# Gate logits from the tenth tile on: outputs as the stationary operand, eight moving columns, summed in place

## The chip, the cores and the metric

The kernel runs on one core of one Trainium2 chip. The metric is the device time of one execution in microseconds (us); less is better.

## The reference, cut to what matters

Two stages follow each other. A gated linear attention runs over a sequence of 768 tokens for each of 4 x 8 heads, and its output, seen as 3072 tokens of 384 numbers, goes through a layer of eight experts, of which each token takes the one with the largest logit.

```python
state = alpha[:, :, t, :, None] * state + k_t v_t          # for each of 768 tokens t
y[:, :, t] = einsum('bhd,bhde->bhe', q[:, :, t], state)
x = y.transpose(0, 2, 1, 3).reshape(3072, 384)
logits = x @ w_gate + modality_bias[modality_id]           # 8 logits for each token
e_idx = argmax(logits, axis=1)
gate_w = softmax(logits)[e_idx]
out[mask] = gate_w * (relu(x[mask] @ w1[e]) @ w2[e])       # for each expert e
```

The change is in `x @ w_gate`.

## The kernel before, in words

The 3072 tokens are 24 tiles of 128. The attention works on two tiles at once: there are 12 pairs, and a loop over s (line 946) has one step for each pair. A step is a software pipeline. In step s the scans of pair s run on VectorE and GpSimd (`back`, `totals`, `forth`, `scaled_keys`, `scaled_queries`), while TensorE makes the scores of pair s - 1 (`scores`), turns its keys (`keys`), and, for pair s - 2, whose outputs have been copied from PSUM to the tile `yt` (`outputs`), turns the outputs into rows for the store (`rows`) and makes the gate logits. Then come `from_state` (queries times the state, tile names qh and UB), `states` (the new state, written to the PSUM tile `kv`) and `from_values` (scores times values, scT and vt). The order on every engine is the order in which the code is written; nothing is moved by a scheduler.

In `yt` the outputs lie turned: head dimension on the partitions, 128 tokens along a row, four blocks j of two heads each, for each of the two tiles c of a pair. The gate weights `wgp` are laid out in the same way, four blocks of 128 x 32 of which 8 columns are filled.

The logits take two stages. `logits_turned` (line 403) makes four matmuls, one for each block j: the weights block (32 columns) is stationary, the outputs of both tiles (256 columns) move, and each result goes to its own 32 partitions of a PSUM bank. ScalarE copies the bank to `lts` (line 408). The four partial sums still have to be added and turned. For the first ten tiles (pairs 0 to 4, `TURNED` = 10) `turn_logits` and a reduction on VectorE do that. For the later tiles (pairs 5 to 11) `add_logits` (line 425) does it with one matmul for each tile: `lts` is stationary and `fold`, a 128 x 8 matrix of ones and zeros made on VectorE at the start (line 200), moves; the result is 8 columns of `LP`, a part of the same PSUM bank as `kv`.

Pairs 5 to 9 get their logits in steps 7 to 11. Pairs 10 and 11 get theirs in the code after the loop, where l = 11 (lines 1091 to 1130): `logits_turned(l - 1)` stands before `from_state(l)` and `add_logits(l - 1)` behind it; `logits_turned(l)` is called between the two halves of the first block of the first expert (line 1123, tiles xHL and w1H, w1L), and `add_logits(l)` after `rows(l)`.

From LP the routing reads the logits on VectorE (`route_group`, tile room), counts tokens per expert on TensorE (`rank_counts`, tiles oh, tri, ones) and from that come the places of the tokens and the choice of the expert weights to load. Behind it 12 blocks of 256 tokens go through the experts.

The PSUM tiles `b` rotate over five banks; `logits_turned` takes one of them in each step. `st[s, "yt"]` has two buffers.

Of the kernel before, what the change touches and what calls it, by code (L numbers as in the profile page):

```python
# [8 lines left out]
F32 = mybir.dt.float32  # L9
# [5 lines left out]
ALU = mybir.AluOpType  # L15
AF = mybir.ActivationFunctionType
AX = mybir.AxisListType
# [4 lines left out]
P = 128  # L22
B, H, S, D = 4, 8, 768, 48
NC = S // P
NP = H // 2
SEG = P + 1
DM = H * D
E = 8
# [26 lines left out]
TURNED = GROUPS[0][1]  # L55
# [20 lines left out]
def attention_moe(ctx: ExitStack, tc: tile.TileContext, q, k, v, alpha, at_, kt_, qt_, vt_, mid, wg, wgp_, mb, w1, w2, out):  # L76
    nc = tc.nc
    order = [1]
    vec, act, pool, pe, sp = (Ordered(e, tc, order) for e in (nc.vector, nc.scalar, nc.gpsimd, nc.tensor, nc.sync))
# [6 lines left out]
    ident = cp.tile([P, P], F32, name="ident")  # L86
# [3 lines left out]
    ac = actx.enter_context(tc.tile_pool(name="ac", bufs=1))  # L90
# [24 lines left out]
    st = {}  # L115
# [14 lines left out]
    def small(p, *shape):  # L130
        return ps.tile([p, *shape], F32, name=next_bank())

    def load(s, names="akqv"):
        z = {"0": slice(0, NP), "1": slice(NP, KS)}.get(names[-1], slice(0, KS))
        for n in names:
            if n == "a":
                c = slice(z.start and z.start * SEG + 1, z.stop * SEG + 1)
                sp.dma_start(X[s % NX_][:, c], at_[s, :, c])
            elif n in "kq":
                sp.dma_start((KT if n == "k" else QT)[s % NB][:, z], (kt_ if n == "k" else qt_)[s, :, z])  # L140
            elif n == "v":
                sp.dma_start(VT[s % NV][:, : 2 * DM], vt_[s])
# [3 lines left out]
    wgp = cp.tile([P, NP, 32], F32, name="wgp")  # L146
# [11 lines left out]
    LP = kvl[:, KS * D :].rearrange("p (t e) -> p t e", e=E)  # L158
# [37 lines left out]
        UB.append(t)  # L196
    bhi = ac.tile([P, 1], F32, name="bhi")
    vec.memset(bhi, -float(ALPHA_MAX_BITS))
    fold = ac.tile([P, E], F32, name="fold")
    vec.tensor_reduce(fold, ident.rearrange("p (j e) -> p e j", e=32)[:, :E], axis=AX.X, op=ALU.add)  # L200
    gacc = ac.tile([P, PS], F32, name="gacc")
    amin = ac.tile([P, PS, KS], F32, name="amin")
    junk = ea.tile([P, KS * SEG + 1], BF16, name="junk")
# [46 lines left out]
    def back(s, z):  # L250
        x, G = X[s % NX_], st[s, "G"]
        r = slice(z.start * SEG + 1, z.stop * SEG + 1)
        vec.tensor_tensor_scan(G[:, r][:, ::-1], x[:, r][:, ::-1], DR[:, ::-1], 0.0, op0=ALU.mult, op1=ALU.max)

    def totals(s, z):
        r = slice(z.start * SEG + 1, z.stop * SEG + 1)
        vec.reciprocal(DF[:, 0::SEG], st[s, "G"][:, r][:, 0::SEG])
# [5 lines left out]
    def scaled_keys(s, z, engine):  # L263
        engine.tensor_tensor(st[s, "k"][:, z], KT[s % NB][:, z], seg(st[s, "G"][:, 1:], 1, z), op=ALU.mult)
# [4 lines left out]
    def begin(s):  # L269
        st[s, "G"] = sb.tile([P, KS * SEG + 1], F32, name="G")  # L270
        st[s, "F"] = ea.tile([P, KS * SEG], F32, name="Fw", bufs=1)
        st[s, "k"] = sb.tile([P, KS, P], F32, name="kh")
        st[s, "q"] = sb.tile([P, KS, P], F32, name="qh")
# [110 lines left out]
    def outputs(s, zs=(0, 1)):  # L384
        if 0 in zs:
            st[s, "yt"] = sb.tile([P, 2, NP, P], F32, name="yt")
        for z in zs:
            act.copy(st[s, "yt"][:, z], st[s, "yp"][z])
# [14 lines left out]
    def logits_turned(s):  # L403
        lt = small(P, 2, P)
        for j in range(NP):
            pe.matmul(lt[32 * j : 32 * j + 32], wgp[:, j], st[s, "yt"][:, :, j], start=True, stop=True)
        l2 = sb.tile([P, 2, P], F32, name="lts")
        act.copy(l2, lt)
        st[s, "l"] = l2
# [14 lines left out]

    def add_logits(s):
        for c in range(2):
            pe.matmul(LP[:, 2 * s + c - TURNED], st[s, "l"][:, c], fold, start=True, stop=True)

    def logits_pe(i, xs, wgs):
        xt = bank(ND, P)  # L430
# [459 lines left out]
    def run(s, phase):  # L890
        for f, a in later.pop((s, phase), ()):
            f(*a)
# [44 lines left out]
    def do(steps):  # L937
        for f in steps:
            f[0](*f[1:])

    def warm(n):
        w = bank(NP, P)
        for i in range(n):
            pe.matmul(w[:, i % NP], ident, ident, start=True, stop=True)

    for s in range(PS):
        if 0 < s and s + 1 < PS:
            load(s + 1, "kqv")
        if 0 <= s - 2:
            outputs(s - 2)  # L950
        late, by = [], vec
        if s == 0:
            warm(14)
            begin(0)
            for z in ZS:
                back(0, z)
                scaled_keys(0, z, pool)
                totals(0, z)
                forth(0, z)
                scaled_queries(0, z, pool if z == Z0 else vec)  # L960
        elif s == 1:
            begin(1)
            scores(0, 0)
            for z in range(2):
                turn_keys(0, z)
                if z == 0:
                    warm(2)
            back(1, Z0)
            scaled_keys(1, Z0, pool)
            scores(0, 1)  # L970
            totals(1, Z0)
            forth(1, Z0)
            scaled_queries(1, Z0, pool)
            back(1, Z1)
            scaled_keys(1, Z1, pool)
            totals(1, Z1)
            forth(1, Z1)
            scaled_queries(1, Z1)
        else:
            if (s - 1, "S") not in st:  # L980
                state(s - 1)
            decayed(s - 1)
            run(s, "state")
            for z in range(2):
                scores(s - 1, z)
            run(s, "masks")
            todo = scans(s)
            if len(todo) > 1:
                late = todo.pop()
            if s >= 4:  # L990
                by = pool
            for f in todo:
                do(f)
            run(s, "counts")
        if 1 < s:
            keys(s - 1)
        if 0 <= s - 2:
            rows(s - 2)
        if 0 <= 2 * (s - 3) < TURNED:
            turn_logits(s - 3)  # L1000
        if 0 <= s - 2:
            logits_turned(s - 2)
        run(s, "small")
        if 0 <= 2 * (s - 3) < TURNED:
            sum_logits(s - 3)
        run(s, "middle")
        do(late[:-1])
        if 0 <= s - 1:
            from_state(s - 1)
        if 0 <= s - 1 and (s - 1) % NC == 0:  # L1010
            states(s - 1)
        if TURNED <= 2 * (s - 2):
            add_logits(s - 2)
        if 0 <= s - 1 and (s - 1) % NC:
            states(s - 1)
        run(s, "sums")
        for f, *x in late[-1:]:
            f(*x, by)
        if 0 <= s - 1:
            from_values(s - 1)  # L1020
        run(s, "end")
        for c in range(s - (s < 5), s + 1 - (s < 4)):
            if 0 <= c < PS:
                guard(c)
        if 0 <= s - 2:
            store(s - 2)
        for c in range(s + 2 + (s > 4), s + 3 + (s > 3)):
            if c < PS:
                load(c, "a")
        if s == 0:  # L1030
            sp.dma_start(wgp, wgp_)
        if s == 1:
            sp.dma_start(mi.rearrange("p t w -> p (t w)"), mid.bitcast(I32))
            sp.dma_start(mbb, mb.unsqueeze(0).broadcast_to([P, NM, E]))
        if s == 2:
            sp.dma_start(xd[MID : MID + 1], of[0:1])
            sp.dma_start(gd[MID : MID + 1], of[0:1, 0:1])
# [37 lines left out]
    def first_block(i, w1, between=None, low_last=False):  # L1075
        xH, xL = XH[i % 2], XL[i % 2]
        wH, wL = w1
        hp = bank(2, T)
        for z in range(2):
            if z and between:  # L1080
                between()
            fs = slice(z * P, (z + 1) * P)
            terms = [[(wH, xH, d), (wL, xH, d), (wH, xL, d)] for d in range(ND)]
            terms = [t for u in terms for t in u]
            if low_last:
                terms.sort(key=lambda t: t[1] is xL)
            for n, (w, x, d) in enumerate(terms):
                pe.matmul(hp[:, z], w[:, d, fs], x[:, d], start=(n == 0), stop=(n == len(terms) - 1))
        return hp

    l = PS - 1
# [4 lines left out]
    w1s = [w1_part(0, 0)]  # L1096
# [3 lines left out]
    slot_tables()  # L1100
    out_of_range()
    rows(l - 1)
    logits_turned(l - 1)
    gate_rows(0, EARLY[0])
    gather_gates(0, row(EARLY[0]))
    store(l - 1)
    with tc.issue_after(sp.last):
        weights(0, 0, (1,))
    from_state(l)
    add_logits(l - 1)  # L1110
    prep(0, False)
    from_values(l)
    route_group(*t[0])
# [6 lines left out]
    rank_masks(*t[0])  # L1120
    w1s += [w1_part(0, 1)]
    outputs(l, (1,))
    hp = first_block(0, w1s[0], lambda: logits_turned(l), True)
    rank_split(*t[0])
    keys_early(1)
    half_index()
    w1s += [w1_part(0, 2)]
    rows(l)
    store(l)
    add_logits(l)  # L1130
    route_places(*t[0])
    act.activation(hf[0], hp, AF.Relu)
    route_group(*t[1])
# [1 line left out]
    hp = first_block(0, w1s[1])  # L1135
# [3 lines left out]
    hp = first_block(0, w1s[2])  # L1139
# [9 lines left out]
    hp = first_block(0, w1s[3], last_counts)  # L1149
# [146 lines left out]
    w1s = []  # L1296
    for u in range(2):
        us = slice(u * P, (u + 1) * P)
        op = py.tile([P, 512], F32, name=f"y{u}")[:, :DM]
        for f in range(NF):  # L1300
            j, z = divmod(f, 2)
# [18 lines left out]
    for i in range(1, NS0):  # L1320
        w1s = slot(i, w1s)
# [90 lines left out]
```

## Time and profile before

| | us |
|---|---|
| runs, as listed | 343.24, 549.6, 344.5 |
| median of the runs | 344.5 |
| the profiled execution | 343.79 |
| its span, from the first to the last instruction | 342.1 |
| TensorE busy (share of the span) | 330.8 (97%) |
| weight loads of TensorE | 300.7 (88%) |
| VectorE busy | 265.7 (78%) |
| ScalarE busy | 229.5 (67%) |
| GpSimd busy | 170.8 (50%) |
| mean granted clock of TensorE, full = 1 | 0.996 |

In the profile's rows PE is TensorE's matmul, PEld its weight load (the two overlap), DVE is VectorE, ACT is ScalarE, POOL is GpSimd. Times are counted from the start of the span. A row of the timeline has the start, the time from the first start to the last end of the instructions merged in it, and their count. One matmul of plain f32 operands shows as two weight loads and two matmul records; a transpose shows as one of each. The matmuls overlap their neighbours, and their ends are modelled, so the time that a group of matmuls takes from the engine is read from its start to the start of the next group, which is called its slot here. All instructions that the recording helper issues have line L66, so the tiles' names tell them apart.

### The profile page before, as it was taken

The page shows a single profiled execution, that of the slowest core. Times are in us where ns is not written, and L with a number is a line of the kernel's source. Part 1 is how long each engine was busy: PE and PEld are TensorE (multiplying, and loading weights), DVE is VectorE, ACT ScalarE, POOL GpSimd, SP SyncE. Part 2 cuts the span into 40 slices and gives each one's busy share as a digit, 9 for nine tenths or more (in the row PEclk, how much of TensorE's full clock was granted, in tenths as well). Part 3 has the DMA queues.
Part 4 walks back from the last instruction along what each step waited for, and adds up shares of the span by engine and source line. Part 5 has one row for each costly group of instructions (what it writes and reads, how often), then busy time and mean ns, then how long its engine had stood idle before and what let it go on. Part 6 is the DMA issues. An engine that isn't in the chain of part 4 may idle for free. (4 is left out here: it accounts for less than half of the span.)

```text
span 342.1 us, 8364 instructions
## 1 busy us (share of the span) xinstructions
PE 330.8 (97%) x3162; PEld 300.7 (88%) x3162; DVE 265.7 (78%) x487; ACT 229.5 (67%) x454; POOL 170.8 (50%) x185
## 2 busy tenths in 40 slices
PE   6899999999999999999999999999999999999991
PEld 6788888888888977999999999999898989898990
DVE  6999999999985876959696868686878777787430
ACT  1767978767686516858585868686868676767430
POOL 7778799788767047554252524251444252411021
PEclk9999999999999999999999999999999999999998
DMA  7998899986185956997867676667586767660010
GB/s 231 398 398 297 288 321 321 327 297 248 44 283 148 375 215 229 372 383 253 258 217 231 210 248 225 227 223 219 164 295 219 223 209 246 205 208 23 1 50 32
DMA packets 39799, 80.07 MB, mean 234 GB/s; under 512 B 3867, under 2 KB 20404, under 8 KB 39748
## 3 DMA queue, kind: packets, MB, share of 16 engines
q1 hardware_dynamic: 35652, 69.38, 58.8%
q0 software_dynamic: 4096, 10.05, 8.9%
q8 instruction: 27, 0.44, 0.5%
q14 instruction: 24, 0.20, 0.2%
HBM read 69.77 MB, written 9.65 MB: 232 GB/s over the span
## 5 line engine op out<-in xcount | busy, mean ns | idle before, releaser
L66 PE MATMUL b<-xHL,w1H 128*128 128x512 f32 (+1 forms) x312 | 102.6, 378 | 0.0
L66 POOL DMA_INDIRECT out_dram<-os,idx x25 | 27.2, 1087 | 110.4 <-ACT os L66 70.8
L66 PE MATMUL b<-xHL,w1L 128*128 128x256 f32 x288 | 80.6, 280 | 0.0
L66 PEld LDWEIGHTS b<-xHL,w1H 128*128 128x128 f32 x312 | 57.4, 188 | 11.3 <-issue 0.4
L66 PE MATMUL y<-w2H,hH 128*128 128x384 f32 x184 | 62.6, 340 | 0.0
L66 PE MATMUL y<-w2H,hL 128*128 128x384 f32 x184 | 61.7, 335 | 0.0
L66 PE MATMUL y<-w2L,hH 128*128 128x384 f32 x184 | 61.6, 335 | 0.0
L66 DVE TENSOR_TENSOR hs<-b,low 128x256 f32<-128x256 f32 x88 | 33.9, 415 | 32.6 <-ACT low L66 32.6
L66 PEld LDWEIGHTS b<-xHL,w1L 128*128 128x128 f32 x288 | 54.2, 188 | 0.1
L66 DVE TENSOR_TENSOR w1L<-w1r,w1H 128x768 fp32r<-128x768 f32 x48 | 43.8, 951 | 6.6 <-ACT w1H L66 6.3
L66 DVE TENSOR_TENSOR w2L<-w2r,w2H 128x768 fp32r<-128x768 f32 x48 | 45.8, 958 | 3.4 <-ACT w2H L66 3.4
L66 ACT ACTIVATE os<-y,gg 128x384 f32<-128x384 f32 x25 | 14.6, 583 | 39.7 <-PE y L66 39.7
L66 ACT CAST w2H<-w2r 128x768 fp32r<-128x768 f32 x48 | 40.0, 841 | 0.0
L66 ACT COPY low<-b 128x256 f32<-128x256 f32 x88 | 30.1, 367 | 14.5 <-PE b L66 14.5
L66 POOL DMA_INDIRECT xg<-xd,idx x26 | 29.4, 1130 | 18.7 <-DVE idx L66 11.0
L66 ACT CAST w1H<-w1r 128x768 fp32r<-128x768 f32 x48 | 37.9, 839 | 0.8 <-ACT ls L66 0.8
L66 POOL DMA_INDIRECT gg<-gd,idx x26 | 28.7, 1103 | 18.7 <-issue 13.1
L66 PEld LDWEIGHTS y<-w2L,hH 128*128 128x128 f32 x184 | 34.6, 188 | 0.0
L66 PEld LDWEIGHTS y<-w2H,hH 128*128 128x128 f32 x184 | 34.6, 188 | 0.0
L66 PEld LDWEIGHTS y<-w2H,hL 128*128 128x128 f32 x184 | 34.5, 188 | 0.0
L66 ACT COPY scT<-b 128x512 f32<-128x512 f32 x48 | 24.8, 599 | 14.2 <-PE b L66 13.1
L66 POOL TENSOR_TENSOR kh<-kt,G 128x512 f32<-128x512 f32 x24 | 30.5, 1278 | 6.3 <-DVE G L66 5.7
(180 smaller groups left out, 593.7 us busy)
## 6 DMA issues: line engine op xcount, KB each, us to landing
w1r<-in_w_dram SPq DMA_DIRECT2D x26, 768.0 KB, 5.4
w2r<-in_w_dram SPq DMA_DIRECT2D x26, 768.0 KB, 5.8
X<-in_turned_alpha_dram SPq DMA_DIRECT2D x10, 516.5 KB, 5.3
kt<-in_turned_k_dram SPq DMA_DIRECT2D x10, 512.0 KB, 5.5
qt<-in_turned_q_dram SPq DMA_DIRECT2D x10, 512.0 KB, 6.6
vt<-in_paired_v_dram SPq DMA_DIRECT2D x12, 384.0 KB, 6.2
xd<-xs SPq DMA_DIRECT2D x12, 384.0 KB, 4.9
kt<-in_turned_k_dram SPq DMA_DIRECT2D x4, 256.0 KB, 2.8
```

The costliest lines, as they stand in the source:

```text
L66: ins = f(*a, **kw)
```

## The change

`add_logits` makes the logits of a tile in one stage. For each of the two tiles c it issues four matmuls, one for each block j, into the same 8 columns of `LP`: the outputs `yt[:, c, j]` (128 x 128) are stationary, 8 columns of the weights block move, and PSUM adds the four. `fold` goes away, and for pairs 5 to 11 so do `logits_turned`, its bank and ScalarE's copy to `lts`. The call stands where `logits_turned` stood: in steps 7 to 11 right after `rows`, that is before `from_state` and `states`; after the loop before `gate_rows` and `from_state(l)` for pair 10, and in the middle of the first expert block for pair 11. Pairs 0 to 4 keep their stages.

```diff
-    fold = ac.tile([P, E], F32, name="fold")
-    vec.tensor_reduce(fold, ident.rearrange("p (j e) -> p e j", e=32)[:, :E], axis=AX.X, op=ALU.add)
...
     def add_logits(s):
         for c in range(2):
-            pe.matmul(LP[:, 2 * s + c - TURNED], st[s, "l"][:, c], fold, start=True, stop=True)
+            for j in range(NP):
+                pe.matmul(
+                    LP[:, 2 * s + c - TURNED], st[s, "yt"][:, c, j], wgp[:, j, :E], start=(j == 0), stop=(j == NP - 1)
+                )
...
-        if 0 <= s - 2:
+        if 0 <= 2 * (s - 2) < TURNED:
             logits_turned(s - 2)
+        if TURNED <= 2 * (s - 2):
+            add_logits(s - 2)
...
-        if TURNED <= 2 * (s - 2):
-            add_logits(s - 2)
         if 0 <= s - 1 and (s - 1) % NC:
             states(s - 1)
...
     rows(l - 1)
-    logits_turned(l - 1)
+    add_logits(l - 1)
...
     from_state(l)
-    add_logits(l - 1)
...
-    hp = first_block(0, w1s[0], lambda: logits_turned(l), True)
+    hp = first_block(0, w1s[0], lambda: add_logits(l), True)
...
     store(l)
-    add_logits(l)
```

TensorE in step 7, the first that changes, before: the partial logits stand ahead of the new state (kv from vt and knat), and the folding behind it.

```order
L66 MATMUL b_1126<-ident,lts 128x128 x2
L66 MATMUL b_1129<-yt,wgp 32x256 x4
L66 MATMUL kv<-vt_89,knat 64x48 x16
L66 MATMUL kv<-fold,lts 128x8 x2
L66 MATMUL b_1141<-scT,vt_89 64x128 x8
```

And now:

```order
L66 MATMUL b_1124<-ident,lts 128x128 x2
L66 MATMUL kv<-wgp,yt 128x8 x8
L66 MATMUL kv<-vt_89,knat 64x48 x16
L66 MATMUL b_1140<-scT,vt_89 64x128 x8
L66 MATMUL b_1141<-scT,vt_89 64x128 x8
```

Four matmuls of 256 columns and two of 8 have become eight of 8 columns, and all stand ahead of the new state.

TensorE after the loop, pair 11, inside the first expert block (b from xHL and the weights w1H, w1L), before:

```order
L66 MATMUL b_2014<-xHL_107,w1H 128x256 x3
L66 MATMUL b_2024<-yt,wgp 32x256 x4
L66 MATMUL b_2014<-xHL_107,w1H 128x256
L66 MATMUL b_2014<-xHL_107,w1L 128x256
L66 MATMUL b_2014<-xHL_107,w1H 128x256
L66 MATMUL b_2014<-xHL_107,w1L 128x256
L66 MATMUL b_2014<-xHL_107,w1H 128x256
L66 MATMUL b_2014<-xHL_107,w1L 128x256
L66 MATMUL b_2014<-xHL_107,w1H 128x256 x3
L66 MATMUL b_2061<-ident,yt 128x128 x4
L66 MATMUL b_2067<-ident,yt 128x128 x4
L66 MATMUL kv<-fold,lts 128x8 x2
```

And now:

```order
L66 MATMUL b_2006<-xHL_107,w1H 128x256 x3
L66 MATMUL kv<-wgp,yt 128x8 x8
L66 MATMUL b_2006<-xHL_107,w1H 128x256
L66 MATMUL b_2006<-xHL_107,w1L 128x256
L66 MATMUL b_2006<-xHL_107,w1H 128x256
L66 MATMUL b_2006<-xHL_107,w1L 128x256
L66 MATMUL b_2006<-xHL_107,w1H 128x256
L66 MATMUL b_2006<-xHL_107,w1L 128x256
L66 MATMUL b_2006<-xHL_107,w1H 128x256 x3
L66 MATMUL b_2054<-ident,yt 128x128 x4
L66 MATMUL b_2060<-ident,yt 128x128 x4
```

The final logits of pair 11 are complete before the second half of that block; the folding behind the transposes of yt is gone.

## Rows read from the trace of the kernel before

**Rows 1.** Page, part 1: busy us (share of the span), instructions.
```profile
PE 330.8 (97%) x3162; PEld 300.7 (88%) x3162; DVE 265.7 (78%) x487; ACT 229.5 (67%) x454; POOL 170.8 (50%) x185
```

**Rows 2.** Busy time by stretch: attention and routing; the expert blocks.
```profile
core 0: us, PE busy (x) PEld busy (x) DVE busy (x) ACT busy (x) POOL busy (x), PEclk, DMA share, GB/s
17.00:125.00 108.00, 108.00 (x1762) 93.90 (x1761) 96.37 (x203) 76.67 (x166) 78.56 (x82) 1.00 0.80 282
...
140.00:330.00 190.00, 190.00 (x1135) 179.54 (x1134) 141.58 (x234) 135.20 (x258) 66.06 (x60) 1.00 0.64 214
```

**Rows 3.** Timeline of PE, step 7.
```profile
start us, us, engine line op out<-in xcount [idle before <-releaser]
...
60.80 0.64 PE L66 MATMUL b<-yt,wgp 128*32 128x256 f32 x8
61.37 1.14 PE L66 MATMUL kv<-vt,knat 128*64 128x48 f32 x32
62.44 0.61 PE L66 MATMUL kv<-fold,lts 128*128 128x8 f32 x4
62.98 0.33 PE L66 MATMUL b<-scT,vt 128*64 128x128 f32 x2
```

**Rows 4.** Timeline of PE after the loop: pair 10, then pair 11.
```profile
104.75 0.64 PE L66 MATMUL b<-yt,wgp 128*32 128x256 f32 x8
105.31 0.28 PE L66 MATMUL b<-ident,gt 128*16 128x128 f32 x1
...
106.56 0.61 PE L66 MATMUL kv<-fold,lts 128*128 128x8 f32 x4
107.02 0.30 PE L66 MATMUL b<-ident,xg 128*128 128x128 f32 x1
...
111.19 0.64 PE L66 MATMUL b<-yt,wgp 128*32 128x256 f32 x8
111.76 0.38 PE L66 MATMUL b<-xHL,w1H 128*128 128x256 f32 x1
...
113.81 0.51 PE L66 MATMUL kv<-fold,lts 128*128 128x8 f32 x4
114.17 0.36 PE L66 MATMUL b<-xHL,w1H 128*128 128x256 f32 x1
```

**Rows 5.** Timeline of PEld: folding in step 7, token table in step 11.
```profile
62.44 0.52 PEld L66 LDWEIGHTS kv<-fold,lts 128*128 128x128 f32 x4
...
96.84 0.47 PEld L66 LDWEIGHTS <-OL 128*128 128x128 f16 x16 [0.41 <-DVE OHE L66]
```

**Rows 6.** Groups by tile, 60 to 115 us: busy us, mean ns | idle before.
```profile
L66 PEld LDWEIGHTS kv<-fold,lts 128*128 128x128 f32 x28 | 3.7, 190 | 0.9 <-issue 0.7 <-ACT lts L66 0.2
L66 ACT COPY lts<-b 128x256 f32<-128x256 f32 x7 | 3.2, 454 | 1.1 <-PE b L66 1.1
```

**Rows 7.** Timeline of PE, steps 2 and 3: transposes before another array split, and before their like.
```profile
18.87 1.04 PE L66 MATMUL b<-ident,yt 128*128 128x128 f32 x8
19.83 0.64 PE L66 MATMUL b<-yt,wgp 128*32 128x256 f32 x8
...
27.18 1.04 PE L66 MATMUL b<-ident,yt 128*128 128x128 f32 x8
28.06 0.38 PE L66 MATMUL b<-ident,lts 128*128 128x128 f32 x2
```

**Rows 8.** Timeline, step 8: VectorE's last read of kv, TensorE's partial logits.
```profile
66.85 0.55 DVE L66 COPY S<-kv 128x384 f32<-128x384 f32 x1
...
68.76 0.64 PE L66 MATMUL b<-yt,wgp 128*32 128x256 f32 x8
```

**Rows 9.** Timeline of PE, step 11: scores; stretch after TensorE's last matmul.
```profile
92.39 2.06 PE L66 MATMUL b<-qh,kh 48*128 48x128 f32 x32
94.38 1.09 PE L66 MATMUL b<-ident,kh 128*128 128x128 f32 x8
...
338.00:342.10 4.10, 0.00 (x0) 0.00 (x0) 0.00 (x0) 0.00 (x0) 0.00 (x0) 0.65 0.03 7
```

## Prediction

> **What bounds the kernel now.** I read the page's shares first: TensorE has the largest, 97% of the span [rows 1]. A busy share can mislead, because matmuls are pipelined and their ends are modelled, so I went on to the busy time by stretch. From 17 to 125 us, where all of the change lies, TensorE is busy for 108.00 of 108.00 us, and from 140 to 330 us for 190.00 of 190.00 [rows 2]. VectorE has 96.37 of the 108 and is a close second. What settles it is the timeline of TensorE: each group of matmuls begins where the one before it leaves off, with no idle bracket, and the same group takes the same slot wherever it stands. The partial logits take 0.57 us in step 7 (60.80 to 61.37) and 0.57 us after the loop (111.19 to 111.76) [rows 3, 4]. An engine that waited now and then for VectorE, a bank or a transfer would show uneven slots. So TensorE's stream of matmuls sets the pace all the way, the expert blocks begin when it gets there, and what a step adds to or takes from the stream arrives at the end one for one. The reader is to see two things: the matching slots, and that nothing else in the program has to change for the time to change.
>
> **What goes.** In steps 7 to 11 the partial logits take 0.57 us and the folding 0.54 us (62.44 to 62.98) [rows 3]; the row of step 7 stands for five equal ones. That is 5 x 1.11 = 5.55 us. For pair 10 it is 0.56 us (104.75 to 105.31) and 0.46 us (106.56 to 107.02); for pair 11 it is 0.57 us and 0.36 us (113.81 to 114.17) [rows 4]. Together 5.55 + 1.02 + 0.93 = 7.50 us leave TensorE's stream.
>
> **What comes.** Each of seven pairs gets eight matmuls of 128 x 128 stationary and 8 moving columns in f32. The trace before has this very shape: the folding, 128*128 with 128x8. Its two matmuls show as four weight loads and four records, so eight will show as sixteen. The four loads last 0.52 us from first start to last end [rows 5], and one load lasts 190 ns [rows 6], so a load starts (0.52 - 0.19) / 3 = 0.11 us after the one before. That weight load is the price; the 8 columns pass beside it. Sixteen of them take 16 x 0.11 = 1.76 us, and seven pairs 7 x 1.76 = 12.32 us. Put simply, the old form loaded little and moved much (weights of 32 columns, four side by side in the array), the new one loads much and moves little, and here loading is the dearer part.
>
> Bounds for the one load, since sixteen in a row of this form do not stand in the trace: the nearest row below is the token table's, f16 128*128, sixteen loads in 0.47 us, 0.03 us each [rows 5]; above is a load that overlaps nothing, 0.19 us [rows 6]. By the lower, seven pairs take 3.4 us, by the upper 21.3. I take 0.11, the row of the same type and shape.
>
> **Edges between groups.** The eight transposes of `yt` take 0.96 us when the partial logits follow, which split the array into four (18.87 to 19.83), and 0.88 us when full-width transposes follow (27.18 to 28.06) [rows 7]. The new matmuls are full width, so the edge before them costs about 0.09 less, seven times: -0.63 us. Behind them, the folding's slot of 0.54 is 0.10 more than four times 0.11, where a split group follows; the new block has such a follower in steps 7 and 9: +0.2 us. Elsewhere full-width or small groups follow, and `from_state` now passes straight into `states`, an edge that I set to nothing between 0 and 0.1.
>
> **The sum.** 12.32 + 0.2 - 7.50 - 0.63 = +4.4 us. Against the profiled execution, 343.79 us (a span of 342.1 and 1.7 around it), that gives 348.2 us. This execution lies between the two undisturbed runs, 343.24 and 344.5, so it serves as the median too. With the lower bound of the load the sum is -4.5 us (339.3), with the upper +13.4 us (357.2).
>
> **What I cost at nothing.** ScalarE loses seven copies to `lts`, 3.2 us [rows 6], but TensorE does not wait for ScalarE in these steps, so nothing is gained. The reduction for `fold` at the start goes, on VectorE, before its first scan; nothing is late for it. The logits of a pair are final before `from_state` instead of behind it, which lets VectorE's routing start sooner, but TensorE reaches the counts no sooner. One bank fewer in the rotation of five only loosens waits. One wait is new: the first of the eight matmuls writes to the bank of `kv`, and so waits for VectorE's last read of it. In step 8 that read ends at 66.85 + 0.55 = 67.40 and the matmul would start near 68.7, 1.3 us later [rows 8]. The whole of TensorE is queued behind that matmul; were the cover gone, each us of lateness would cost a us. TensorE getting slower widens it.
>
> **Rivals.**
>
> The load goes at the short pace, and the change gains. The matmul has only 8 columns to move, and if the stationary operand could be taken in as the f16 table is, 0.03 us for each [rows 5], the time would be 339.3 us. For it: that row is real, and the same engine does it. Against: the folding, in f32, has 0.11 four times over, and the operand here is f32. The Trainium skill, "TensorE: Matmul & The Clock Gate", section "Back-to-back issue gap", gives a floor of about 25 ns for an isolated matmul of few columns, which would speak for this rival, but says that in a stream of loads and matmuls both set the spacing; the folding's row agrees with the second.
>
> TensorE is not the bound, and the added time is hidden: 343.8 us, no difference. For it: VectorE is busy for 96.37 of 108 us [rows 2], and PE's ends are modelled, so TensorE's wait could be hidden in overlaps. Against: the equal slots. It would need slots that shrink when the matmuls come earlier.
>
> The clock falls, and the kernel is slower by more than 2%. In steps 8, 10 and 11 there would stand, one after the other, the transposes of keys and of outputs, eight each (0.88 us for eight [rows 7]), and 1.76 us of matmuls with few columns: some 3.5 us with little moving, against 1.8 us now before the partial logits, which move 256 columns each. The granted clock does fall in this trace: it is 0.65 on average from 338 to 342 us, where TensorE has nothing to do [rows 9]. If it fell to the lower of its two levels (1.2 against 2.4 GHz) in one such step while the values and scores pass, the scores alone, 1.99 us (92.39 to 94.38) [rows 9], would take twice that, and the values, of like length, too: about +3.9 us a step. One full fall gives 352.1 and decides it; five give 367.7. Against: the clock is 1.00 over all stretches with work [rows 2], and TensorE is never idle. The same page, section "Part 4: PE-mode transpose", says that transposes do not count as activity in the way that matmuls do. No run here shows that; by it this rival gets a little more weight, still a small one.
>
> **How the numbers follow.** The forecast, 348.2 us, gets 0.87. The clock gets 0.05, the hidden cost 0.05, the short load 0.03. A measurement of this kernel tells about 2% from no change, 6.9 us, so from 337.6 to 351.4 us is the middle class. The forecast lies in it at +1.3%, the hidden cost and the short load's 339.3 too; of the latter I put 0.02 beyond the edge, since its 0.03 us counts the last load's whole length in. Of the forecast 0.03 goes to the upper side, for waits at the new place. So faster 0.02, same 0.90, slower 0.08. The range is 345.5 to 351.0 us: below, it takes in a load that overlaps a little better and half of the hidden case; above, a load of 0.13 us or edges twice as dear.
>
> **What would show it.** Right: each of the seven blocks of eight matmuls shows sixteen loads at 0.11 us and a slot of 1.75 to 1.9 us, TensorE still fills its stretch, the scores' slot is still 1.99 us, and the first expert block starts about 4.4 us later with all behind it moved by as much. Wrong: a slot of the block under 1 us (short load), idle brackets on TensorE or unequal slots (a wait has taken over), a granted clock under 1.00 between 60 and 115 us, or a later part that takes up the delay.

## Result and the profile after

The changed kernel takes 347.64 us (median of 4 runs, 345.95 to 349.69). The kernel before has a median of 343.87 us over four runs; one of them, 549.6 us, stands far from all others, and the ratio leaves it out. The other three have a median of 343.24 us, and against them the changed kernel takes 1.0127 times as long, with a 95% interval of 1.0099 to 1.0155. Run a second time among the experiments it gave 1.010 (1.0068 to 1.0132). It is slower by a little over 1%, which the rule of 2% calls no change, and the interval lies clear of 1. The prediction was 348.2 us, a ratio of 1.013.

The first thing to look at is where TensorE's time went. This is its timeline in step 7 of the changed kernel, the same stretch as [rows 3]:

```profile
60.19 0.38 PE L66 MATMUL b<-ident,lts 128*128 128x128 f32 x2
60.41 1.85 PE L66 MATMUL kv<-wgp,yt 128*128 128x8 f32 x16
62.19 1.14 PE L66 MATMUL kv<-vt,knat 128*64 128x48 f32 x32
63.16 0.51 PE L66 MATMUL b<-scT,vt 128*64 128x128 f32 x6
```

Eight matmuls show as sixteen records, and their slot is 60.41 to 62.19, 1.78 us, where partial logits and folding took 0.57 and 0.54. Step 11 and the two places after the loop, the latter beside [rows 4]:

```profile
97.87 1.85 PE L66 MATMUL kv<-wgp,yt 128*128 128x8 f32 x16
99.58 0.54 PE L66 MATMUL b<-OHE,OL 128*128 128x2 f16 x16
...
106.83 1.85 PE L66 MATMUL kv<-wgp,yt 128*128 128x8 f32 x16
108.53 0.27 PE L66 MATMUL b<-ident,gt 128*16 128x128 f32 x1
...
113.86 1.85 PE L66 MATMUL kv<-wgp,yt 128*128 128x8 f32 x16
115.57 0.36 PE L66 MATMUL b<-xHL,w1H 128*128 128x256 f32 x1
```

Here the slots are 1.71, 1.70 and 1.71 us. The loads, beside [rows 5] and [rows 6], from PEld's timeline in step 7 and from the groups by tile between 60 and 118 us:

```profile
60.30 1.87 PEld L66 LDWEIGHTS kv<-wgp,yt 128*128 128x128 f32 x16
```

```profile
L66 PEld LDWEIGHTS kv<-wgp,yt 128*128 128x128 f32 x112 | 13.1, 192 | 0.0
```

Sixteen loads in 1.87 us, each of 0.192: (1.87 - 0.19) / 15 = 0.112 us from one to the next. The busy time by stretch, beside [rows 2]:

```profile
core 0: us, PE busy (x) PEld busy (x) DVE busy (x) ACT busy (x) POOL busy (x), PEclk, DMA share, GB/s
17.00:128.00 111.00, 111.00 (x1787) 101.36 (x1784) 95.81 (x202) 74.45 (x159) 79.45 (x83) 1.00 0.78 274
143.00:333.00 190.00, 190.00 (x1134) 179.50 (x1134) 141.69 (x234) 135.25 (x257) 68.49 (x61) 1.00 0.65 216
```

TensorE still fills every stretch and its clock is full. PEld's busy time in the first stretch has grown from 93.90 to 101.36 us, in a stretch 3 us longer: what the change adds is loading.

A good measure of the whole is TensorE's own way from one fixed group to its last matmul, because it leaves out the start (first loads from memory) and the end (last store), which vary from run to run. From the transposes of `yt` in step 2 to the last matmul of the last expert block, the kernel before and then the changed kernel. For the latter a row between stands here too, the first expert block behind the last changed group, which in [rows 4] starts at 114.17 us:

```profile
18.87 1.04 PE L66 MATMUL b<-ident,yt 128*128 128x128 f32 x8
...
334.29 0.34 PE L66 MATMUL y<-w2H,hL 128*128 128x384 f32 x1
```

```profile
18.57 1.04 PE L66 MATMUL b<-ident,yt 128*128 128x128 f32 x8
...
117.52 0.37 PE L66 MATMUL b<-xHL,w1H 128*128 128x256 f32 x1
...
337.64 0.34 PE L66 MATMUL y<-w2H,hL 128*128 128x384 f32 x1
```

The way is 315.42 us before and 319.07 us after: +3.65 us. This is the effect of the change as TensorE sees it, 1.1% of the time, and the measured ratios agree with it. All of it arises up to the row between: from there to the last matmul TensorE takes 220.12 us in both kernels (114.17 to 334.29, 117.52 to 337.64), so the expert blocks pass the delay on one for one. The profiled execution's own time rose by only 345.95 - 343.79 = 2.2 us; its start was 0.30 us earlier (18.57 against 18.87), and the stretch from the last matmul's start to the end of the span 1.3 us shorter (6.5 against 7.8). The end is not touched by the change. At the start the reduction for `fold` is gone, but the same row starts at 18.57 to 19.18 us in the runs below that have no `fold` either, so the 0.30 us are within what varies.

### The profile page after: what moved, and what is told of

The parts are those of the page before. It is cut to its first block, busy times and chain, and to the rows that moved or that the text cites. A ratio compares the mean times of both kernels' runs of the same rounds, so it can differ in the third digit from the quotient of the medians.

```text
span 344.1 us, 8411 instructions
## 1 busy us (share of the span) xinstructions
PE 335.0 (97%) x3190; PEld 309.1 (90%) x3190; DVE 265.5 (77%) x486; ACT 227.7 (66%) x447; POOL 172.2 (50%) x185
## 4 chain that ended last, share of the span: by engine, by line
PE 91%; DVE 3%; DMA 2%; issue 1%; SPq 0%; ACT 0%; POOL 0%; POOLq 0%; DVEq 0%
PE b L66 54%; PE y L66 30%; PE kv L66 8%; DMA X<-in_turned_alpha_dram 1%; DVE Fw L66 1%; DVE G L66 1%; DMA out_dram<-os,idx 1%; DVE qh L66 1%; SPq L66 0%; POOL out_dram L66 0%; DVE room L66 0%; ACT os L66 0%; POOLq L1324 0%; ACT hH L66 0%; DVEq L66 0%
## 5 line engine op out<-in xcount | busy, mean ns | idle before, releaser
L66 POOL DMA_INDIRECT xg<-xd,idx x26 | 31.3, 1205 | 20.9 <-DVE idx L66 11.0
L66 ACT COPY scT<-b 128x512 f32<-128x512 f32 x48 | 24.8, 598 | 13.9 <-PE b L66 13.4
```

The costliest lines, as they stand in the source:

```text
L66: ins = f(*a, **kw)
```

## Experiments

**The block once more, in the same place.** Each pair's eight matmuls are issued twice. This prices sixteen loads and asks whether added work is hidden.

```diff
-        for c in range(2):
+        for c in (0, 1, 0, 1):
             for j in range(NP):
                 pe.matmul(
```

> The changed kernel with each block of eight logit matmuls issued a second time into the same columns (same result). If TensorE's stream sets the pace and a 128x128 f32 weight load costs 0.11 us, each of seven pairs gets sixteen more loads, 16 x 0.11 = 1.78 us: all that stands behind moves by 7 x 1.78 = 12.4 us more than in the changed kernel, the time is about 360 us (ratio 1.047 to 1.052 to the kernel before), and the scores keep their slot of 1.99 us. If the added work is partly hidden (VectorE or a later part takes it up), the ratio stays under 1.035. If long stretches of transposes and 8-column matmuls make the clock fall, the granted clock is under 1.00 between 60 and 125 us, the scores' slot rises toward 4 us and the ratio is above 1.06.

Measured: 373.0 us, ratio 1.0897 (1.085 to 1.0944): far above the 360 us that the loads alone would give. The mean granted clock of its four runs is 0.947 to 0.958. Busy time by stretch, and the timeline of TensorE in step 8:

```profile
61.00:65.00 4.00, 4.00 (x48) 3.98 (x48) 3.56 (x6) 2.28 (x6) 3.07 (x3) 1.00 1.00 361
65.30:68.60 3.30, 3.30 (x42) 3.30 (x40) 3.10 (x9) 0.59 (x1) 2.03 (x3) 0.50 0.94 327
...
75.50:82.20 6.70, 6.70 (x92) 6.29 (x93) 4.18 (x11) 0.00 (x0) 2.38 (x3) 0.50 0.76 273
60.00:145.00 85.00, 85.00 (x1072) 81.03 (x1071) 50.77 (x126) 38.84 (x81) 38.98 (x44) 0.84 0.53 179
```

```profile
71.05 1.09 PE L66 MATMUL b<-ident,kh 128*128 128x128 f32 x8
71.97 1.04 PE L66 MATMUL b<-ident,yt 128*128 128x128 f32 x8
72.85 4.44 PE L66 MATMUL kv<-wgp,yt 128*128 128x8 f32 x32
...
77.70 1.99 PE L66 MATMUL b<-qh,UB 64*64 64x128 f32 x32
79.62 1.95 PE L66 MATMUL kv<-vt,knat 128*64 128x48 f32 x32
```

The column behind POOL's is the granted clock. It is 1.00 at first and 0.50, the lower of the two levels (1.2 against 2.4 GHz), from 65.3 and from 75.5 us, though TensorE is busy without a gap (4.00 of 4.00). Before the second fall TensorE did eight transposes of keys, eight of outputs and then only loads with 8 columns behind each. What follows pays: `from_state` takes 1.92 us (77.70 to 79.62) in place of the 1.03 that it takes in the run with wide operands below. Over 60 to 145 us the mean clock is 0.84, so 0.16 x 85 = 13.6 us of full-speed work were lost. TensorE's way, from 19.18 to its last matmul at 363.21 us, is 344.03 us, 25.0 more than the changed kernel's. Seven pairs at 1.78 us make 12.5 of it; the remaining 12.5 is near the 13.6 of the clock. So the added work is not hidden, and the falling clock, one of the prediction's rivals, is real: it shows with two blocks a pair in this place, and not in the two profiles with one.

**The same loads with wide operands.** This run tells the added work from what it moves. Eight more matmuls with the same stationary operands follow each block, but 128 columns of the identity move, into a bank that nothing reads.

```diff
                     LP[:, 2 * s + c - TURNED], st[s, "yt"][:, c, j], wgp[:, j, :E], start=(j == 0), stop=(j == NP - 1)
                 )
+        w = bank(2, P)
+        for c in range(2):
+            for j in range(NP):
+                pe.matmul(w[:, c], st[s, "yt"][:, c, j], ident, start=(j == 0), stop=(j == NP - 1))
```

> The changed kernel, and behind each block eight more f32 matmuls with the same stationary operands, but 128 columns of the identity moving in place of 8, into a bank that nothing reads. Loads are as many as in the run that issued the block twice, and each is 0.11 us there. If what lets the clock fall is a long stretch in which few columns move, and not the added work, the granted clock stays 1.00 from 18 us to TensorE's last matmul, the added eight take about 1.75 us and the time is 7 x 1.75 = 12 us above the changed kernel, about 360 us (ratio 1.044 to 1.050). If stretches of f32 loads as such, or the added time, let it fall, the granted clock falls as in that run and the ratio is 1.07 to 1.10.

Measured: 359.72 us, ratio 1.0457 (1.043 to 1.0484). Timeline of TensorE in step 8, and the busy time by stretch:

```profile
70.83 1.85 PE L66 MATMUL kv<-wgp,yt 128*128 128x8 f32 x16
72.54 2.03 PE L66 MATMUL b<-ident,yt 128*128 128x128 f32 x16
74.40 0.20 PE L66 MATMUL b<-oh,tri 128*128 128x80 bf16 x1
...
74.81 1.10 PE L66 MATMUL b<-qh,UB 64*64 64x128 f32 x32
75.84 1.14 PE L66 MATMUL kv<-vt,knat 128*64 128x48 f32 x32
```

```profile
60.00:130.00 70.00, 70.00 (x1045) 66.66 (x1044) 48.79 (x119) 36.20 (x76) 39.36 (x44) 1.00 0.55 188
17.00:340.00 323.00, 323.00 (x3079) 298.30 (x3076) 248.55 (x462) 215.90 (x427) 154.79 (x150) 1.00 0.68 229
```

The clock stays at 1.00, and the means of its four runs are 0.993 to 0.996. The added matmuls take 1.86 us (72.54 to 74.40), though sixteen times as many columns move: the load and the 128 columns pass beside each other. TensorE's way (18.71 to 350.82 us, 332.11) is 13.04 us above the changed kernel's. The seven added groups have slots of 1.79 to 1.96 us, 13.16 in all, and in steps 7 and 9 the block ahead of them is 0.07 shorter than in the changed kernel: together 13.02. That is the cleanest statement in this study that TensorE's stream sets the time: what was added to it came out one for one. The loads are as many as in the run before and the time that they take is nearly equal (1.86 us against 1.78 a pair), but the clock fell in that run and not in this one, where 128 columns moved behind half of the loads. So neither the number of loads nor the added time alone is what made it fall.

**The second block apart from the first.** The added work is that of the first run, but its second half stands where the folding stood.

```diff
+        if TURNED <= 2 * (s - 2):
+            add_logits(s - 2)
         if 0 <= s - 1 and (s - 1) % NC:
             states(s - 1)
...
     from_state(l)
+    add_logits(l - 1)
     prep(0, False)
...
     store(l)
+    add_logits(l)
     route_places(*t[0])
```

> The changed kernel with each block issued twice into the same columns (same result), but the second time where the folding stood: behind from_state, for pair 11 behind rows. The added work is that of the run that issued the block twice in one place; only from_state (or the rest of the expert block) stands between. If the clock falls for stretches without dense matmuls, it falls less often here: ratio 1.05 to 1.07, with falls in the records at most where only short groups stand between the two blocks. If it answers to the amount of such work, whatever stands between, the ratio is that of the other run, 1.085 to 1.094.

Measured: four runs of 372.42, 370.2, 364.12 and 370.81 us, median 370.51; their mean granted clocks are 0.961, 0.967, 0.982 and 0.966. The first of them is the profiled one. Its busy time by stretch:

```profile
65.00:71.80 6.80, 6.80 (x58) 6.45 (x59) 5.52 (x12) 1.20 (x3) 2.14 (x3) 0.50 0.76 265
60.00:137.00 77.00, 77.00 (x987) 73.35 (x985) 43.45 (x94) 35.24 (x75) 38.77 (x44) 0.82 0.49 163
```

The clock falls here as well, for as much in sum (0.18 x 77 = 13.9 us). The expectation that about one us of `from_state` between the blocks would keep the clock up was wrong: three of the four runs took as long as the runs with both blocks in one place (371.4 to 376.18 us) or about 1 us less, and only one, 364.12 us, came out where falls were to be rarer. What differs between the four runs is the clock. Their spans of 370.6, 368.4, 362.3 and 369.0 us, each times its mean clock, are 356.1, 356.2, 355.8 and 356.5 us: within 0.7 us of each other, where the spans differ by 8.3. So in the fastest run the clock was down for less time; where it fell in that run no profile shows.

**The old place.** The eight matmuls stand where the folding stood, and nowhere else.

```diff
-        if TURNED <= 2 * (s - 2):
-            add_logits(s - 2)
         run(s, "small")
...
+        if TURNED <= 2 * (s - 2):
+            add_logits(s - 2)
         if 0 <= s - 1 and (s - 1) % NC:
             states(s - 1)
...
-    add_logits(l - 1)
     gate_rows(0, EARLY[0])
...
     from_state(l)
+    add_logits(l - 1)
...
-    hp = first_block(0, w1s[0], lambda: add_logits(l), True)
+    hp = first_block(0, w1s[0], None, True)
...
     store(l)
+    add_logits(l)
```

> The changed kernel's eight matmuls, but called where the folding stood: behind from_state in steps 7 to 11 and for pair 10, and after rows for pair 11. If only the matmuls and the edges between groups count, TensorE still never idles, the blocks keep 1.7 to 1.85 us, the edges cost 0.1 us more in each step, and the first expert block's second half starts 0.3 to 0.8 us later than in the changed kernel (ratio 1.010 to 1.018 to the kernel before). If the earlier place is what lets VectorE's routing keep up, idle brackets of TensorE appear near the counts after the loop, and the time rises by 1 us or more over that.

Measured: 350.76 us, ratio 1.0211 (1.0176 to 1.0246). Timeline of TensorE in step 9, then ScalarE and TensorE in step 10 and the loads of 90.95 to 91.03 us there, and what follows the block of step 7, with the busy time there:

```profile
79.96 1.04 PE L66 MATMUL b<-ident,yt 128*128 128x128 f32 x8
80.93 1.10 PE L66 MATMUL b<-qh,UB 64*64 64x128 f32 x32
81.96 1.95 PE L66 MATMUL kv<-wgp,yt 128*128 128x8 f32 x16
83.84 0.37 PE L66 MATMUL kv<-vt,knat 128*64 128x48 f32 x5
```

```profile
89.83 1.12 ACT L66 COPY knat<-b 128x512 f32<-128x512 f32 x2
90.73 1.37 PE L66 MATMUL b<-qh,UB 64*64 64x128 f32 x32
92.03 1.95 PE L66 MATMUL kv<-wgp,yt 128*128 128x8 f32 x16
```

```profile
91.00 0.15 PEld L66 LDWEIGHTS b<-qh,UB 64*64 64x64 f32 x4
```

```profile
63.46 3.51 PE L66 MATMUL b<-scT,vt 128*64 128x128 f32 x32
```

```profile
63.70:67.10 3.40, 3.40 (x34) 3.07 (x32) 3.18 (x9) 0.68 (x2) 2.18 (x2) 0.50 0.87 293
```

TensorE's way (18.57 to 341.03 us, 322.46) is 3.39 us longer than the changed kernel's. One fall of the clock, 3.4 us long, accounts for 1.65 of them: the values in step 7 take 3.44 us in place of 1.86, and the scores behind them 2.06 in place of 1.99. The other 1.7 us, 0.24 a pair, is more than the 0.3 to 0.8 in all that I expected, and it has two parts. The larger, some 1.1 us, is edges: between two groups that split the array the block takes 1.88 us (81.96 to 83.84), and the transposes ahead of a split group take 0.97 (79.96 to 80.93). The smaller, 0.6 us, is waiting: `from_state` takes 1.16, 1.30 and 1.09 us in steps 8, 10 and 11 and 1.20 for pair 10, where the changed kernel has 1.03 or 1.04 each time. In step 10 its loads stop after the first four and go on at 91.00 us, 0.05 after ScalarE's copy of the keys ends (89.83 + 1.12 = 90.95); in the other three places they go on 0.05 us after a copy of ScalarE's too. No idle bracket of TensorE's matmuls shows it, since their records overlap; the uneven slots do. So the earlier place helps by its full-width neighbours, and by the time that the block gives ScalarE to copy before `from_state`. No wait for VectorE's routing shows.

**Half words.** Behind each block the same eight matmuls follow on the upper halves of the f32 words, read as bf16, into spare columns.

```diff
+        spare = kvl[:, 496:512].rearrange("p (t e) -> p t e", e=E)
+        y16, w16 = (t.bitcast(BF16) for t in (st[s, "yt"], wgp))
+        for c in range(2):
+            for j in range(NP):
+                pe.matmul(spare[:, c], y16[:, c, j, 1::2], w16[:, j, 1 : 2 * E : 2], start=(j == 0), stop=(j == NP - 1))
```

> The changed kernel, and behind each block the same eight matmuls once more on the upper half words of the outputs and weights, read as bf16 (every second element), into spare columns that nothing reads. If the price of a load is that of its type (0.03 us in the f16 token table), each pair gets eight loads in 0.25 to 0.4 us and the time rises by 2 to 3 us over the changed kernel (ratio about 1.020). If the price is that of 128 columns whatever the type, or of the step of two between elements, it is eight times 0.11, 0.9 to 1.0 us a pair, +6 to +7 us (ratio about 1.032). A rise of over 10 us would say that one load takes as long as in f32 with both passes.

Measured: 350.27 us, ratio 1.02 (1.0167 to 1.0232). The two forms merge in one row of TensorE's timeline, here in step 8 and for pair 11; below them the busy time after pair 11's block:

```profile
69.41 2.05 PE L66 MATMUL kv<-wgp,yt 128*128 128x8 f32 x24
71.32 0.20 PE L66 MATMUL b<-oh,tri 128*128 128x80 bf16 x1
...
115.11 0.52 PE L66 MATMUL b<-xHL,w1H 128*128 128x256 f32 x3
115.47 2.05 PE L66 MATMUL kv<-wgp,yt 128*128 128x8 f32 x24
117.37 0.43 PE L66 MATMUL b<-xHL,w1H 128*128 128x256 f32 x1
```

```profile
117.60:120.90 3.30, 3.30 (x18) 3.30 (x17) 3.04 (x12) 0.48 (x1) 0.00 (x0) 0.50 1.06 373
```

Both together take 1.91 us (69.41 to 71.32), so the eight bf16 matmuls add 0.20 us to the 1.71, as the f16 row of [rows 5] has it: 0.025 us each, even with a step of two between elements, and one record each where f32 has two. The price of the block is that of the f32 type. The ratio came out as expected, but only about half for the reason given: seven times 0.20 is 1.4 us, and one fall of the clock after pair 11's block costs 1.55 (from 117.37 us on, seven groups of the expert block and the transposes behind them take 3.50 us, where the changed kernel takes 1.95). Together that is 2.95, and TensorE's way (18.98 to 341.01 us, 322.03) is 2.96 us above the changed kernel's. Ahead of this fall TensorE did no transposes but matmuls of the expert block, which move 256 columns, and then 1.90 us of matmuls with 8 columns.

**Only the neighbours.** The kernel before, its two stages kept, in other places: partial logits behind the scores, folding behind the transposes.

```diff
             for z in range(2):
                 scores(s - 1, z)
+            if TURNED <= 2 * (s - 2):
+                logits_turned(s - 2)
...
-        if 0 <= s - 2:
+        if 0 <= 2 * (s - 2) < TURNED:
             logits_turned(s - 2)
+        if TURNED <= 2 * (s - 2):
+            add_logits(s - 2)
...
-        if TURNED <= 2 * (s - 2):
-            add_logits(s - 2)
...
         scores(l, z)
+    logits_turned(l - 1)
...
     rows(l - 1)
-    logits_turned(l - 1)
+    add_logits(l - 1)
...
     from_state(l)
-    add_logits(l - 1)
```

> The kernel before with its two stages for the late pairs in other places: the partial logits right behind the scores, among groups that split the array, and the folding right behind the transposes for rows, among full-width groups (steps 7 to 11 and pair 10; pair 11 as before). The same matmuls, only other neighbours. If edges between array splits cost about 0.1 us each and TensorE's stream sets the pace, each step is 0.2 to 0.35 us shorter (the folding's slot falls from 0.54 to 0.36-0.44, the edge before the partial logits from 0.20 to the 0.20 that the scores have anyway), 1.2 to 1.8 us in all: ratio 0.995 to 0.997. If the folding has to wait for ScalarE's copy, which now stands behind the copies of the scores, TensorE shows waits of up to 0.5 us a step and the ratio is 1.000 to 1.008.

Measured: 342.46 us, ratio 0.9973 (0.9956 to 0.9991), the one version below both kernels. By the rule of 2% that is no change, and the interval is only just clear of 1. Timeline of TensorE in step 9, and of its loads for pair 10:

```profile
75.45 0.64 PE L66 MATMUL b<-yt,wgp 128*32 128x256 f32 x8
76.02 1.09 PE L66 MATMUL b<-ident,kh 128*128 128x128 f32 x8
76.95 1.04 PE L66 MATMUL b<-ident,yt 128*128 128x128 f32 x8
77.83 0.51 PE L66 MATMUL kv<-fold,lts 128*128 128x8 f32 x4
78.27 1.10 PE L66 MATMUL b<-qh,UB 64*64 64x128 f32 x32
```

```profile
103.86 0.52 PEld L66 LDWEIGHTS kv<-fold,lts 128*128 128x128 f32 x4 [0.16 <-ACT lts L66]
```

The folding's slot is 0.44 us (77.83 to 78.27) in place of 0.54, and the transposes of `yt` take 0.88 (76.95 to 77.83) in place of 0.97. In steps 7 to 11 no wait for `lts` shows. For pair 10 there is one: the folding's loads begin only when ScalarE's copy to `lts` is done, and pair 10 gains nothing. TensorE's way (18.80 to 332.86 us) is 314.06 us, 1.36 less than before, with the same matmuls in it; the five steps' slots account for all of it (0.33, 0.28, 0.19, 0.27 and 0.28 us).

**The changed kernel once more.**

> The changed kernel itself, once more. If its first profile is typical, TensorE's last matmul starts 3.3 to 3.7 us later than in the kernel before, the granted clock does not fall before TensorE is done, and the ratio is 1.010 to 1.014. If it stands near the edge at which the clock falls, some executions hold one fall of about 1.7 us: a spread of the times of 2 us or more above the lowest, and perhaps a fall in this profile too.

Measured: ratio 1.010 (1.0068 to 1.0132), six runs from 345.89 to 349.02 us. TensorE's way in this profile is 319.07 us (18.71 to 337.78), the same to 0.01 as in the first, and the clock does not fall. The spread of 3.1 us is above the 2 us that I had set as a sign of a fall in single runs, but the kernel before spreads as much (342.22 to 344.95 in 17 and 11 runs), so the spread decides nothing. The slowest run of the changed kernel, 349.69 us, has a mean clock of 0.988, and no run of the kernel before is on record under 0.992. That points to a fall in that run, but a longer end at the low clock would lower the mean too, and no profile of it shows which.

## Why the prediction was right

TensorE as the bound: right. The change itself came out at the end to 0.01 us, and so did the added wide matmuls (13.04 against 13.02) and the moved ones (1.36 against 1.35). VectorE, 96.37 of 108 us busy, is in no wait of TensorE's between 60 and 125 us of the changed kernel.

What goes, 7.50 us: taken from the rows of before, and gone.

What comes, 12.32 us: the load at 0.11 us is right (0.112). The blocks' slots are 1.78 in step 7 and in step 9 (78.57 to 80.35 us) and 1.70 or 1.71 elsewhere, which is just under the 1.75 to 1.9 that was to show the forecast right: 12.1 in all, where the prediction had 12.32 + 0.2 = 12.5 with the edges behind. A block takes less than sixteen times its load because only fifteen of these distances lie between its first and its last matmul, 1.68 us; the next group starts 0.02 to 0.03 us later, or 0.10 where it splits the array.

Edges: -0.63 was right in sign and size for the side before the block (0.09 or 0.10 us in each of the seven places, 0.67 in all). `from_state` passing straight into `states` cost nothing, as set (1.04 us in step 8, 70.91 to 71.95, as before). What the prediction left out are the edges that went with the folding, about 0.25 us. In step 7 `states` no longer stands before it and takes 0.97 us (62.19 to 63.16) where it took 1.07 (61.37 to 62.44 [rows 3]), and the values behind it take 1.86 where they took 1.90. In pair 11's expert block the transposes that stood before the folding take 0.79 (116.73 to 117.52) where they took 0.88, and the expert's first matmul behind the logits is 0.02 shorter.

With all of them, 12.09 - 7.51 - 0.67 - 0.25 = 3.66 us, against 3.65 measured on TensorE and 4.4 predicted. The terms that were mis-sized are the block's own slot, by 0.4 us, and the edges, by 0.3, both to the same side. That the medians of the first comparison lie 4.4 us apart (347.64 and 343.24), just as forecast, is luck: in the second it is 2.8 (346.73 and 343.94).

Costs at nothing: right. The new wait for VectorE's read of `kv` did not show, and the sum of the slots leaves nothing for ScalarE's seven copies saved.

Rivals. The short load did not come: f32 pays 0.11 us, bf16 0.025, in the same place. The hidden cost did not come. The clock did not fall in the two profiles of this kernel (1.00 from 17 to 128 us). I gave that 0.05, and the argument against it that TensorE is never idle was wrong: TensorE shows no gap where the clock fell, either. That the forecast held on this point is in part luck, for the same eight matmuls had one fall in the old place. The rival's price, 3.9 us for a fall, is near that of the longer falls of the doubled blocks (6.7 us at half speed, 75.50 to 82.20, so some 3.4 us lost) and twice that of the shorter ones (1.65 us in the old place, 1.55 with half words). The Trainium skill, "TensorE: Matmul & The Clock Gate", section "Part 4: PE-mode transpose", says that a transpose does not count as activity in the way that a matmul does. The runs bear on it only in part. In steps 8 to 11 of the changed kernel sixteen transposes and then the block stand in a row, and the clock stayed at 1.00 in both profiles. In the old place `states` stands between the transposes and the block of step 7, and with half words matmuls of 256 columns stand ahead of pair 11's; there it fell. So which stretches let the clock fall stays open.

## What to carry to other kernels

When an engine has no idle time at all, compare the slots of its groups, from start to start, in one trace: here they gave the price of a change to 0.7 us in 344, and a shape that already occurs prices one that will. A matmul with a full f32 stationary operand and few moving columns cost its weight loads here, 0.112 us each, and with 128 columns behind the same loads the group took 1.86 us in place of 1.78; so put the smaller operand on the stationary side, or many columns behind each load. Where several such forms stand in a row, look at the granted clock. And see which groups stand next to each other: moving one beside others that split the array and one beside others of full width saved 1.36 us without removing an instruction. An uneven slot tells of a wait even where the engine shows no idle time.

## What was not expected of the hardware

The granted clock fell to half (from 2.4 to 1.2 GHz) while TensorE was busy without a gap: mean 0.84 over 85 us when each pair issued thirty-two f32 loads with 8 columns behind each, 1.00 when sixteen of them had 128 columns behind them. It fell once each in the profiles of two kernels close to the changed one: the same matmuls in the old place, and eight short bf16 matmuls (0.20 us) more for each pair. A change of this form can thus lose more than its loads say, and the clock of every run has to be looked at.

An edge between a full-width group and one that splits the array cost about 0.1 us in each of the seven places ahead of the block (in steps 8 to 11 0.96 or 0.97 against 0.87 or 0.88 for the same transposes), and moving two groups of matmuls to better neighbours, with nothing else changed, gave 1.36 us.
